# A launch with idle products and second-stage tables in two parts, in a kernel of a Fourier layer and a gated two-layer network

## The chip, the cores and the metric

The kernel runs on one core of a Trainium2 chip. The metric is the device time in microseconds (us). Differences are judged against executions of the kernel before on the same chip. TensorE does the matrix products, VectorE and ScalarE copy and compute, GpSimd and SyncE issue the loads and stores.

## The reference

For 8 batches of 3072 x 256 numbers, a real Fourier transform along the 3072, a complex 256 x 256 mixing with a bias and a shrinkage, the inverse transform, and then a gated two-layer network on neighbouring rows:

```python
X = np.fft.rfft(x, axis=1)
Yr = Xr @ w_r - Xi @ w_i + b_r
Yi = Xr @ w_i + Xi @ w_r + b_i
# shrink each by lam = 0.01
y = np.fft.irfft(Yr + 1j * Yi, n=x.shape[1], axis=1)
# the second half, on y as x
x_prev = x shifted by one row
k = np.maximum((mu_k * x + (1 - mu_k) * x_prev) @ w_k, 0.0)
out = sigmoid((mu_r * x + (1 - mu_r) * x_prev) @ w_r) * (k * k @ w_v)
```

## The kernel before

The transform is done in two stages by products with tables of sines: a first stage of 96 points, then (for the first two batches by "turns", which are products with an identity) a layout change, then a second stage with a table `G` that the kernel computes at launch. Then come the mixing (16 products per unit), the bias addition `z` with the shrinkage `Y` on VectorE, and the back products with an inverse table `GI`, which is `G` turned by TensorE. Six units `u` of four groups each make one batch.

A small scheduler in Python decides the order of instructions when the program is built: each unit has a due time and needs, copies are given to ScalarE or VectorE by which is estimated to be free first, and four slots of PSUM, the buffer that products are written to, are handed out. The resulting order on each engine is fixed; only the waits are decided on the chip.

The tables and the bias before the change (cuts are marked by dots, and some comments are added here):

```python
reduce_angle(scr[:, 768:2304], N, scr[:, 2304:3840])      # VectorE, 1536 elements
...
for src, p0, p1, g0, g1 in ((b_r, 0, 64, 0, 5), (b_i, 64, 128, 1, 5), (b_i, 65, 128, 0, 1), (b_r, 64, 65, 0, 1)):
    nc.gpsimd.dma_start(out=bias5[p0:p1, g0:g1, :], in_=src...to_broadcast(...))
...
def tables(k):                                            # two sines of 1536 elements
    nc.scalar.activation(G[:, :, :, 0, :], ang, AF.Sin, bias=0.0, scale=sc0)
    at(run_on("act", k, 1.5) + 0.3, tables1)
def tables1(k):
    nc.scalar.activation(G[:, :, :, 1, :], ang, AF.Sin, bias=0.0, scale=sc1)
    at(run_on("act", k, 1.5), tables2)
```

The mixing, what follows it on VectorE, and the back products:

```python
def shrink(k):
    nc.vector.tensor_scalar(out=y, in0=z, scalar1=LAM, scalar2=-LAM, op0=ALU.min, op1=ALU.max)
    nc.vector.tensor_tensor(out=y, in0=z, in1=y, op=ALU.subtract)
...
def back(u):
    def issue(ps, h, end):
        y = Y.pop(u)
        for i in range(4):
            nc.tensor.matmul(ps[:, 256 * i:256 * i + 256], GI[:, 4 * u + i, :],
                             y[:, 256 * i:256 * i + 256], start=True, stop=True)
...
units.append(Unit(f + g, 0.87, [("xt", b, u)] + ([("xt0", b), "bias"] if u == 0 else []), mix(u, 0)))
...
tab += [Unit(18.0 + n, 0.5, ["G", ("x1", 0, 3, 1)], table_gi(n)) for n in range(3)]
```

## Time and profile before

| what | before |
|---|---|
| median of 3 runs | 592.51 us (592.41 to 592.64) |
| span of the traced run | 591.0 us |
| busy: TensorE, VectorE, ScalarE | 96%, 88%, 71% |
| products of the input (128 x 96), mean | 280 ns |
| start of the first bias addition `z` | 25.01 us |
| first VectorE copy of batch 1's turns, "the hand-over" | 44.34 us |

The time is a few tenths of a per cent longer than the span, which runs from the first to the last instruction. The prediction shows the lines that carry most of this. Two more are needed later. The first is from the groups by shape of the kernel before, between 6 and 15 us. Its columns are line, engine, operation, output and inputs, shapes, type and count, then the busy time and the mean ns of one, then idle time before them and what ended it. The second is from its chain of waits (start, length, what).

```profile
L326 PE MATMUL banks<-FT,xs 96*128 96x96 f16 x64 | 5.9, 280 | 2.0 <-DMA xs<-in_x_dram 2.0
```

```profile
28.53 1.75 PE banks L414 x16
```

The input products are slow here: 280 ns each, where those of the same line and shape take 206 ns from 35.4 us on. A later mixing of 16 products takes 1.75 us, at a granted clock of 1.00.

### The profile page before, as it was taken

The numbers are of one execution on the slowest core, as the hardware profiler recorded it, in microseconds if no ns is written. First come the engines' busy times: TensorE is split into PE (matmuls) and PEld (weight loads), VectorE is DVE, ScalarE is ACT, GpSimd is POOL, SyncE is SP. The second block draws the span as 40 slices with busy tenths as digits, with TensorE's granted clock in tenths as the row PEclk, the third lists the DMA queues.
The fourth block names the chain that finished last, engine by engine and source line by source line (L and its number), as shares of the span: only waits on it lengthen the run. The fifth ranks groups of instructions, "written<-read, shape, count | busy, mean of one in ns | idle before, by whom it ended". The sixth has DMA issues, their size and how long they took to land.

```text
span 591.0 us, 12301 instructions
## 1 busy us (share of the span) xinstructions
PE 566.1 (96%) x4822; PEld 429.1 (73%) x4889; DVE 522.4 (88%) x831; ACT 421.0 (71%) x459; POOL 26.7 (5%) x56
## 2 busy tenths in 40 slices
PE   3999999999999999999999999999999999999996
PEld 3888666777767777677777777677876787776665
DVE  7799999789998899898998989988999889979883
ACT  5786967677768677676777677777776867767652
POOL 7101000000000000000000000000000000000000
PEclk9999999999999999999999999999999999999999
DMA  8976978724598265963478655683337722352223
GB/s 134 142 149 161 187 181 231 179 72 106 127 230 234 60 139 143 248 182 78 107 183 245 148 116 130 169 229 107 101 97 232 179 55 73 104 165 71 65 57 94
DMA packets 69594, 84.38 MB, mean 143 GB/s; under 512 B 9121, under 2 KB 54560, under 8 KB 69536
## 3 DMA queue, kind: packets, MB, share of 16 engines
q1 hardware_dynamic: 62912, 68.98, 41.7%
q0 software_dynamic: 6432, 14.36, 16.7%
q8 instruction: 38, 0.62, 0.4%
q10 hardware_dynamic: 192, 0.26, 0.2%
q14 instruction: 20, 0.16, 0.1%
HBM read 50.73 MB, written 47.19 MB: 166 GB/s over the span
## 4 chain that ended last, share of the span: by engine, by line
PE 84%; ACT 6%; DVE 4%; issue 2%; DMA 2%; POOL 0%; SPq 0%; DVEq 0%; POOLq 0%; ACTq 0%
PE banks L670 28%; PE banks L626 24%; PE banks L414 14%; PE banks L653 5%; PE banks L453 4%; PE banks L271 3%; PE banks L386 3%; ACT rl L632 3%; PE banks L534 2%; ACT rg L658 2%; DMA xs<-in_x_dram 1%; PE banks L344 1%; DVE YT L220 1%; DMA out_dram<-o 1%; DVE z L426 1%
## 5 line engine op out<-in xcount | busy, mean ns | idle before, releaser
L632 ACT ACTIVATE rl<-banks 128x1024 bf16<-128x1024 f32 x192 | 193.6, 1029 | 94.3 <-PE banks L626 88.5
L626 PE MATMUL banks<-xk,wk 128*128 128x512 bf16 x701 | 188.7, 379 | 5.3 <-DVE xk L599 0.7
L670 PE MATMUL banks<-wv,k 128*128 128x256 bf16 x1536 | 183.0, 272 | 0.4 <-ACT rl L632 0.3
L670 PEld LDWEIGHTS <-k 128*128 128x128 bf16 x1536 | 149.3, 98 | 29.1 <-issue 1.4
L638 DVE TENSOR_TENSOR k<-rl 128x1024 bf16<-128x1024 bf16 x192 | 130.3, 684 | 13.6 <-ACT rl L632 13.5
L626 PEld LDWEIGHTS <-wk 128*128 128x128 bf16 x768 | 73.9, 98 | 60.7 <-issue 3.1
L414 PEld LDWEIGHTS <-XT 128*128 128x128 bf16 x768 | 74.5, 98 | 16.1 <-DVE XT L396 0.7
L414 PE MATMUL banks<-wi,XT 128*128 128x256 bf16 x384 | 73.3, 273 | 0.1
L414 PE MATMUL banks<-wr,XT 128*128 128x256 bf16 x384 | 73.3, 272 | 0.1
L599 DVE SCALAR_TENSOR_TENSOR xk<-diff,muk,YT 128x512 bf16<-128x512 bf16 x96 | 69.0, 744 | 0.2
L599 DVE SCALAR_TENSOR_TENSOR xr<-diff,mur,YT 128x512 bf16<-128x512 bf16 x96 | 68.7, 744 | 0.0
L681 DVE TENSOR_TENSOR o<-banks,rg 128x1024 f32<-128x1024 f32 (+1 forms) x49 | 58.6, 1195 | 3.7 <-PE banks L670 3.4
L218 ACT ACTIVATE YT<-banks 128x768 bf16<-128x768 f32 x57 | 43.5, 830 | 11.3 <-PE banks L534 7.9
L218 ACT ACTIVATE XT<-banks 128x1024 bf16<-128x1024 f32 (+2 forms) x46 | 43.3, 950 | 10.4 <-PE banks L386 10.4
L653 PE MATMUL banks<-wrm,xr 128*128 128x256 bf16 x384 | 49.8, 272 | 0.1
L658 ACT ACTIVATE rg<-banks 128x1024 bf16<-128x1024 f32 x48 | 49.2, 1025 | 0.0
L431 ACT ACTIVATE z<-banks 128x1024 bf16<-128x1024 f32 x32 | 32.7, 1022 | 19.7 <-PE banks L414 19.6
L653 PEld LDWEIGHTS <-xr 128*128 128x128 bf16 x384 | 37.2, 98 | 11.6 <-issue 0.2
L218 ACT ACTIVATE V<-banks 128x1024 bf16<-128x1024 f32 x35 | 35.9, 1025 | 12.8 <-PE banks L453 12.8
L218 ACT ACTIVATE A<-banks 96x1024 bf16<-96x1024 f32 (+1 forms) x39 | 39.3, 1023 | 7.5 <-PE banks L271 6.2
L593 DVE TENSOR_TENSOR diff<-YT 128x1024 bf16<-128x1024 bf16 x48 | 32.8, 683 | 3.8 <-ACT YT L218 3.8
L220 DVE CAST A<-banks 96x1024 bf16<-96x1024 f32 (+1 forms) x21 | 25.5, 1221 | 11.4 <-PE banks L271 9.4
(90 smaller groups left out, 448.3 us busy)
## 6 DMA issues: line engine op xcount, KB each, us to landing
out_dram<-o SPq DMA_DIRECT2D x188, 128.0 KB, 2.3
xs<-in_x_dram POOLq DMA_DIRECT2D x32, 384.0 KB, 6.5
Vdr<-V SPq DMA_DIRECT2D x192, 64.0 KB, 1.8
V<-Vdr SPq DMA_DIRECT2D x32, 384.0 KB, 7.0
Adr<-A SPq DMA_DIRECT2D x24, 384.0 KB, 5.6
A<-Adr SPq DMA_DIRECT2D x48, 192.0 KB, 4.3
wk<-in_moe_w_k_dram POOLq DMA_DIRECT2D x1, 512.0 KB, 14.1
wv<-in_moe_w_v_dram POOLq DMA_DIRECT2D x1, 512.0 KB, 14.5
```

The lines of the kernel that those rows point to most:

```text
L218: nc.scalar.activation(out, in_, AF.Copy, bias=0.0, scale=1.0)
L414: nc.tensor.matmul(o, lhs, w[:, c, :], start=(w is wr and c == 0), stop=(w is wi and c == NCD - 1))
L431: nc.scalar.activation(z, ps, AF.Copy, bias=0.0, scale=1.0)
L593: nc.vector.tensor_tensor(out=df, in0=y, in1=yp, op=ALU.subtract)
L599: nc.vector.scalar_tensor_tensor(out=m[:, c, :], in0=df[:, c, :], scalar=mu[:, c:c + 1], in1=yp[:, c, :], op0=ALU.mult, op1=ALU.add)
L626: nc.tensor.matmul(ps[:, 512 * f:512 * f + 512], wk[:, c, 128 * ff:128 * ff + 128], xk[:, c, :], start=(c == 0), stop=(c == NCD - 1))
L632: nc.scalar.activation(rl, ps, AF.Relu, bias=0.0, scale=1.0)
L638: nc.vector.tensor_tensor(out=k2, in0=rl, in1=rl, op=ALU.mult)
L653: nc.tensor.matmul(ps[:, 256 * q:256 * q + 256], xr[:, c, 128 * q:128 * q + 128], wrm[:, c, :], start=(c == 0), stop=(c == NCD - 1))
L658: nc.scalar.activation(rg, ps, AF.Sigmoid, bias=0.0, scale=1.0)
L670: nc.tensor.matmul(ps[:, 256 * q:256 * q + 256], K2[t][:, ff, 128 * q:128 * q + 128], wv[:, ff, :], start=(ff == 0), stop=(ff == NCF - 1))
L681: nc.vector.tensor_tensor(out=o[:, lo:hi], in0=ps[:, lo:hi], in1=rg[:, lo:hi], op=ALU.mult)
```

## The change

The intent is to start the body earlier. Products of zeros ("idle products") keep TensorE busy from the launch so that its clock gate is open when the input arrives. By the clock gate I mean what the traces show as two speeds of TensorE, with a granted clock of 0.50 where it is shut and of 1.00 where it is open. In the kernel before, turns of one shape take 289 ns before 19.8 us and products of that shape 218 ns behind it. The opening is its first clock record, at 19.21 us. A gate that is still shut at the launch doesn't show in the granted clock: it reads 1.00 between 13 and 16 us, where the first turns took 305 ns. Half of the second-stage table, which is enough for the first three units, is made first. The other half, the three later turns and the inverse tables are put behind the first mixings. The core of the diff:

```diff
+    idle = const.tile([128, 512], BF16, name="idle")
+    nc.vector.memset(idle, 0.0)
+    def keep_warm(ps, n):
+        for _ in range(n):
+            nc.tensor.matmul(ps[:, 0:512], idle[:, 0:128], idle, start=True, stop=True)
...
-    reduce_angle(scr[:, 768:2304], N, scr[:, 2304:3840])
+    for o in (0, 768):
+        reduce_angle(scr[:, 768 + o:1536 + o], N, scr[:, 2304 + o:3072 + o])
...
+                if b == 0 and c == 1:            # in the pauses between input loads
+                    spare, i = take()
+                    keep_warm(spare, 2 if q < 3 else 1)
+                    release(i, end + 0.5)
...
+            if b == 0 and u > 2:                 # the last three turns wait
+                needs.append(("xt", 0, LATE[u - 3]))
...
+                    if b == 0 and u < 2:         # second half of the sines
+                        at(k, lambda k: tables3(k, u))
...
-                needs = [("y", b, u), "GI"]
+                needs = [("y", b, u), ("GI", u // 2)]
...
-    done["FT"], done["bias"] = 5.0, 21.0
+    done["FT"], done["bias"] = 5.0, 20.0
...
-    tab += [Unit(18.0 + n, 0.5, ["G", ("x1", 0, 3, 1)], table_gi(n)) for n in range(3)]
+    tab += [Unit(18.0 + 3 * n, 0.5, ["G1" if n else "G", ("mixed", 0, 2 * n)], table_gi(n)) for n in range(3)]
...
+    spare, i = take()
+    keep_warm(spare, 14)
+    release(i, 6.0)
```

More of the change, by code (lines that the diff above doesn't have):

```diff
@@ L195 @@
     heap, seq = [], itertools.count()
-    free = {"pe": 0.0, "act": 6.0, "dve": 12.0}
+    free = {"pe": 0.0, "act": 6.0, "dve": 12.7}
     done, slots = {}, {}
@@ L354, in issue @@
                 at(end, evac)
-            return Unit(t1 + (t2 - t1) * u / 6, 0.45, [("x1", b, 3, 0), ("x1", b, 3, 1)], issue)
+            needs = [("x1", b, 3, 0), ("x1", b, 3, 1)]
+            if b == 0 and u > 2:
+                needs.append(("xt", 0, LATE[u - 3]))
+            return Unit(t1 + (t2 - t1) * u / 6, 0.45, needs, issue)
         return [make(q, c) for q in range(4) for c in range(2)] + [turn(u) for u in range(NU)]
     NU = NG // 4
+    LATE = (0, 0, 1)
     def middle(b, t0, t1):
@@ L417, in issue @@
                     return
+                done["mixed", b, u] = end - 0.15
                 z = r1_pool.tile([128, 1024], BF16, name="z")
@@ L501, in middle @@
             if s < NU:
-                units.append(Unit(f, 0.44, [("A2", b, s), "G"], second(s)))
+                units.append(Unit(f, 0.44, [("A2", b, s), "G1" if s > 2 else "G"], second(s)))
             if 0 <= s - 1 < NU:
@@ L727, in evac, with sine @@
                                                 scalar2=None, op0=ALU.mult)
-                if n == 2:
-                    done["GI"] = e
+                done["GI", n] = e
             at(end, evac)
         return issue
+    def sine(hf, j):
+        g = slice(12 * hf, 12 * hf + 12)
+        nc.scalar.activation(G[:, g, :, j, :], ang[:, g], AF.Sin, bias=0.0, scale=(sc0, sc1)[j])
     def tables(k):
-        nc.scalar.activation(G[:, :, :, 0, :], ang, AF.Sin, bias=0.0, scale=sc0)
-        at(run_on("act", k, 1.5) + 0.3, tables1)
+        sine(0, 0)
+        run_on("act", k, 0.85)
+        at(11.6, tables1)
     def tables1(k):
-        nc.scalar.activation(G[:, :, :, 1, :], ang, AF.Sin, bias=0.0, scale=sc1)
-        at(run_on("act", k, 1.5), tables2)
+        sine(0, 1)
+        at(max(14.0, run_on("act", k, 0.85)), tables2)
     def tables2(k):
@@ L744, in tables2, with tables3 @@
         done["G"] = run_on("dve", k, 0.5)
+    def tables3(k, j):
+        sine(1, j)
+        e = run_on("act", k, 0.85)
+        if j == 1:
+            done["G1"] = e
     P = 71.5
@@ L781 @@
     for q in range(4):
-        done["x", 0, q] = 6.0 + 2.55 * q
+        done["x", 0, q] = (6.3, 8.9, 11.0, 12.8)[q]
         load_x(1, q)
@@ L788 @@
     big["wv"] = load_w("wv", moe_w_v, NCF, D)
-    done["FT"], done["bias"] = 5.0, 21.0
-    at(12.0, tables)
+    done["FT"], done["bias"] = 5.0, 20.0
+    at(10.9, tables)
     tab = [Unit(18.0, 0.1, ["FT"], table_fi)]
-    tab += [Unit(18.0 + n, 0.5, ["G", ("x1", 0, 3, 1)], table_gi(n)) for n in range(3)]
+    tab += [Unit(18.0 + 3 * n, 0.5, ["G1" if n else "G", ("mixed", 0, 2 * n)], table_gi(n)) for n in range(3)]
     streams = [tok, val, fa, fb, fc, tab]
     at(START - 10.0, lambda k: mix_tokens(0, k))
+    spare, i = take()
+    keep_warm(spare, 14)
+    release(i, 6.0)
     place, held, t = [0] * len(streams), {}, 0.0
```

## The prediction

> **What bounds the kernel now.** I read the page first. TensorE is busy 96% of 591.0 us and VectorE 88%, so the body is a TensorE pipeline. But the order of instructions of before and after is the same on TensorE, VectorE and ScalarE from the second batch's turns (about 42 us) to the end; only what stands before differs. So the whole effect is a shift of the moment at which that common order begins, and I read only the first 46 us, first in the chain of work that ended last:
>
> ```profile
> 4.10 8.63 DMA xs<-in_x_dram
> 12.77 1.47 PE banks L326 x16
> 14.34 0.97 DVE YT L220
> 15.35 4.18 PE banks L344 x39
> 19.56 0.69 ACT A L218
> ...
> 23.69 1.28 PE banks L414 x10
> 25.01 1.23 DVE z L426
> 26.24 0.02 issue
> 26.26 0.44 DVE Y L442
> 26.70 0.02 issue
> 26.72 0.70 DVE Y L443
> ...
> 43.16 1.13 DVE V L220
> 44.29 0.00 DVEq L220
> 44.29 0.04 issue
> 44.34 1.24 DVE A L220
> ```
>
> (Start, length, what.) The input lands at 12.73 whatever TensorE does. Then come the last first-stage products, the 48 turns (L344), the first mixing (L414), the first bias addition z at 25.01, and at 44.34 the first VectorE copy of batch 1's turns. That copy, 44.34, is the hand-over to the common order: I ask when it comes after the change.
>
> The groups of TensorE by shape, from the stretches 15 to 20 us and 20 to 24 us, show the clock:
>
> ```profile
> L344 PE MATMUL banks<-ident,YT 128*128 128x128 f16 x48 | 4.9, 289 | 0.8 <-ACT YT L218 0.7
> L716 PE MATMUL banks<-ident,G 128*128 128x128 f16 x24 | 1.7, 218 | 0.0
> ```
>
> The same shape takes 289 ns before 19.8 us and 218 ns behind it. The row of granted clock reads 9 everywhere, so it doesn't show this gate.
>
> Last the DMA issues of 5 to 23 us and GpSimd's timeline:
>
> ```profile
> bias<-in_b_i_dram POOLq DMA_DIRECT2D x1, 128.0 KB, 12.8
> bias<-in_b_i_dram POOLq DMA_DIRECT2D x1, 31.5 KB, 12.7
> bias<-in_b_r_dram POOLq DMA_DIRECT2D x1, 0.5 KB, 11.9
> 9.91 0.99 POOL L179 DMA_DIRECT2D bias<-in_b_r_dram  x1
> 21.50 0.73 POOL L170 DMA_DIRECT2D wrm<-in_moe_w_r_dram  x1 [3.79 <-DMA bias<-in_b_i_dram]
> ```
>
> The last number of an issue is the time from its start to its landing (for x: 4.10 + 8.63 = 12.73, and TensorE starts at 12.77). So the bias tile is complete at 9.91 + 11.9 = 21.8 us; GpSimd, which waits for one of its parts, goes on at 21.50. Before, nobody notices: z comes at 25.01.
>
> [...] L344 starts at 14.96 and the fast products start by 19.8; the earlier bursts (1.5 us with gaps of 0.3 to 1.3) did not open it. [...]
>
> **The change part by part.**
> *Idle products.* 14 products of 512 columns, from about 1.1 us (after one memset on an idle VectorE). [...] The first real product waits until 6.28 anyway, so they cost nothing. Two more fill each pause between the loads. If the gate is open at 12.77: 8 products of 96 columns take 0.51 us instead of 0.84 (rows of 35.4 and 9.7 us), so the last 16 end at 13.65, not 14.24. 48 turns at 56 ns instead of 104 ns would save 2.3 us, but only three of the six now stand ahead of the second stage.
>
> *Tables in two parts.* Two sines of 1536 elements (1.58 and 1.56 us) become four of 768, about 0.85 us each, two of them before the second stage. ScalarE has the last x1 copied at about 14.5; VectorE ends its share (copies 12.7 to 14.65, since the six passes of angle reduction together still end near 12.7), then G0 to 15.2. The turns start at 14.7 instead of 15.35. Turn 0 is computed at 15.3 and copied by ScalarE to 16.35; second stage 16.4 to 17.45, two more turns to 18.35; the negations on VectorE stand behind copies of 0.69 and 1.22 us and end at 19.15 and 19.4. The first mixing so ends about 20.3, against 24.97: 4.7 us earlier.
>
> *What this meets.* VectorE has one more copy in front (to 20.6) and could then do z. The bias is there at 21.8. No DMA issue in this stretch waits for work that the change speeds up (they wait for earlier landings), so I take 21.85 for z: 3.15 us earlier than 25.01, not 4.4.
>
> *What is moved behind z.* From z to the hand-over VectorE was busy with almost no pause, 25.01 to 44.34 = 19.3 us. In the order of after the same stretch holds: four z+Y+Y of 2.40 (9.6), two of them with z copied by ScalarE first, 1.8 each (3.6), the halving of GI 0.63, four negations of 0.23 (0.9), one turn copy 1.2, two V copies of 1.22 (2.45), three YT copies of 0.9 (2.7): 21.1 us. So 1.8 us of what used to stand before z now stands behind it. 21.85 + 21.1 = 42.95.
>
> *Waits inside.* TensorE has 24 inverse-table products (0.45 us a group of eight) and one turn in the way now, and four PSUM slots. Following the order by hand I find VectorE idle for about 0.1 us at a negation, 0.4 at the late turn (the third mixing waits for a slot first), 0.2 at the last z, and some 0.1 elsewhere: 0.8 us. Hand-over at 43.75 instead of 44.34: gain 0.6 us. ScalarE, by the same walk, is at its copy of batch 1 at 43.6 instead of 43.82: 0.2 us. So the sum: 4.7 earned, of which 1.5 lost to the bias wait and VectorE's copy, 1.8 to work moved behind, 0.8 to new pauses: 0.6 left. The stretch from 15 to 43 us is worked by hand, with an error of about 1 us, and the author of the change set the bias time to 20 in the schedule, which leans the other way; I move the point to a gain of 1.0: **591.5 us**.
>
> **The rivals.**
> *The bias is not in the way* (it lands earlier, or the first mixing comes later than I think). Then z is at 20.6 and the hand-over at 42.5: gain about 1.8, 590.7 us. For it: a change in order might shift DMA. Against: GpSimd's own wait at 21.50.
> *The whole 4.7 us comes through*, 587.8 us: if TensorE, not VectorE, set the pace from 25 to 44 us. TensorE is nearly full from 28 to 38 (5.00 and 4.88 of 5 us), which speaks for it; VectorE is at 4.95 of 5 in 40 to 45, and the chain there is VectorE, which speaks against.
> *The gate does not open early* (zeros don't count, or the pauses close it). Then the last first-stage products and three turns are slower by 0.6 + 1.2 us, z comes at about 22.4 instead of 21.85: gain 0 to 0.4, 592.3 us. Small, because the bias hides it.
> *New pauses are larger* (slots, inverse tables between back products): another 1 us, 592.9 us, about nothing gained or a little lost.
>
> **Range and chances.** My walk gives 591.9, the first rival 590.7, the full shift 587.8 at small odds, the pauses 592.9. Range 589.8 to 592.8. 2% would be 11.9 us, over twice all that the front could give (the input lands at 12.73 and 45 us is the hand-over), and nothing behind it changes order. Faster by over 2%: 0.01; within: 0.985; slower: 0.005.
>
> **What would show it.** Right: turns of about 218 ns from 14.7; the first mixing done near 20.3; z idle before it, released by the bias DMA, at 21.8; the first VectorE copy of batch 1's turns at 43 to 44; every later row moved by one constant. Wrong: L357 products at 289 ns; z before 21.5 or after 22.5; a hand-over before 42 or after 44.5; or a shift that grows or shrinks after 46 us (a DMA then sets the pace).

Where a cut is marked, the prediction told rules of the hardware that no run of this case shows. Two stand as my assumptions. One is that a waiting `z` holds up everything behind it on VectorE: in the trace of the changed kernel VectorE stands idle for the 1.85 us ahead of `z`, and its next piece of work starts at 23.68 us. The other is an end of the 14 idle products near 6 us: in that trace they end at 6.70 us, the first clock record (1.00) is at 5.90, the first input products start at 6.58 instead of 6.33, and the last ones at 12.76, where before it was 12.77. The 0.85 us for a sine of 768 elements is an estimate from the 1.58 and 1.56 us of the long ones; 0.94 and 0.92 were measured in the changed kernel. The sum: 4.7 less 1.5, 1.8 and 0.8 leaves 0.6 us, and the point was then moved to a gain of 1.0, which makes 591.5. A pause of TensorE that shuts the gate had no term in it.

## The result and the profile after

The changed kernel took 593.16 us (median of 6 runs, 592.70 to 595.16). The kernel before took 592.51 us in the same rounds (592.27 to 593.49). The ratio is 1.0016 with a 95% interval of 0.9999 to 1.0032. Ratios here are the mean time of one kernel's runs over that of the other's of the same rounds, so they are not quite the ratio of the medians quoted. The class "within 2%" was right. The point of 591.5 was not, and the median lies 0.36 us above the range. All outputs are right.

The six times are not one cluster: four lie at 592.70, 592.80, 593.12 and 593.20 us, and two at 594.45 and 595.16. The traced run is the one of 594.45. What its trace shows is therefore first of all the story of a slow one.

**The launch.** The groups by shape of the changed kernel, 0 to 15 us, show the input products:

```profile
L335 PE MATMUL banks<-FT,xs 96*128 96x96 f16 x64 | 3.4, 206 | 2.3 <-DMA xs<-in_x_dram 2.3
```

They take 206 ns instead of 280: the zeros opened the gate. But for one product at 14.25 us, the turns started at 14.85 us (predicted 14.7), and the first mixing ended near 20.4 us (predicted 20.3).

**The bias.** The timeline of the changed kernel (start, length, engine, line, operation, operands, count, then the idle time before it and what ended it) shows the first `z` on VectorE and the first back product on TensorE:

```profile
22.42 1.22 DVE L446 TENSOR_TENSOR z<-banks,bias 128x1024 bf16<-128x1024 f32 x1 [1.85 <-DMA bias<-in_b_i_dram]
...
25.27 0.60 PE L473 MATMUL banks<-Y,GI 128*128 128x256 bf16 x4 [2.08 <-DVE GI L746]
```

VectorE stands idle for 1.85 us until the bias lands, as predicted, but at 22.42 us rather than 21.85. The back product needs `Y`, which needs this `z`, and it also needs the halved row of `GI`, which VectorE does just behind `Y`. So TensorE has nothing to do for 2.08 us. Before, the first back product waited 0.30 us.

**What the pause did.** The chain of waits of the changed kernel (the part from the first `z` to the second inverse table, then the hand-over):

```profile
22.42 1.23 DVE z L446
23.68 0.44 DVE Y L462
24.14 0.69 DVE Y L463
...
25.27 0.60 PE banks L473 x4
25.87 0.45 PE banks L403 x8
26.31 3.22 PE banks L433 x16
29.53 0.65 PE banks L736 x8
...
45.75 1.24 DVE A L229
```

The third mixing (L433, the L414 of before) takes 3.22 us where the kernel before took 1.75 at the line shown above. The windows of the changed kernel tell why. The columns are the stretch, its length, busy us and instruction count of the engines PE, PEld, DVE, ACT and POOL, then the granted clock, the DMA share and GB/s:

```profile
24.00:25.00 1.00, 0.00 (x0) 0.00 (x0) 0.95 (x4) 0.00 (x0) 0.00 (x0) 1.00 1.01 199
...
26.00:27.00 1.00, 1.00 (x12) 0.79 (x10) 0.97 (x2) 1.00 (x2) 0.00 (x0) 0.69 1.13 215
27.00:28.00 1.00, 1.00 (x6) 0.74 (x5) 0.86 (x3) 0.84 (x1) 0.00 (x0) 0.50 1.17 225
...
29.00:30.00 1.00, 1.00 (x11) 0.88 (x10) 0.43 (x1) 0.00 (x0) 0.00 (x0) 0.60 1.13 229
30.00:31.00 1.00, 1.00 (x15) 0.89 (x13) 0.96 (x2) 0.80 (x1) 0.00 (x0) 1.00 1.05 208
```

The granted clock is 0.50 in the middle of it. In finer windows it fell between 26.2 and 26.6 us and was back at 29.8, a stretch of 3.4 us. The pause of 23.19 to 25.27 had closed the gate again. One of the products in this stretch, by shape, 26 to 30 us:

```profile
L433 PE MATMUL banks<-wi,XT 128*128 128x256 bf16 x8 | 2.5, 418 | 0.0
```

It takes 418 ns on average, where the page of the kernel before has 273 for its L414. In all, the hand-over came at 45.75 us, 1.41 later than before.

**Behind the hand-over.** The prediction said that every later row moves by one constant. I compared the start of the first and of the last row of differences (`diff`) in the body. The shift grew from 1.41 to 1.67 us: 0.26 us were added in one place, near 250 us, where TensorE waits for the inverse-stage input of a batch (the load of V) to land. The traced spans differ by 592.7 - 591.0 = 1.7 us.

### The profile page after: what moved, and what is told of

Same layout as the page of the kernel before. It is cut to its first block, busy times and chain, and to the rows that moved or that the text cites. A ratio compares the mean times of both kernels' runs of the same rounds, so it can differ in the third digit from the quotient of the medians.

```text
span 592.7 us, 12418 instructions
## 1 busy us (share of the span) xinstructions
PE 574.1 (97%) x4910; PEld 428.4 (72%) x4910; DVE 523.4 (88%) x837; ACT 421.5 (71%) x461; POOL 25.9 (4%) x56
## 4 chain that ended last, share of the span: by engine, by line
PE 82%; ACT 5%; DVE 4%; DMA 4%; issue 2%; POOL 1%; SPq 0%; DVEq 0%; POOLq 0%; ACTq 0%
PE banks L690 27%; PE banks L646 24%; PE banks L433 14%; PE banks L673 5%; PE banks L473 3%; PE banks L280 3%; PE banks L403 3%; PE banks L554 2%; ACT rl L652 2%; DMA bias<-in_b_r_dram 2%; DMA V<-Vdr 1%; ACT rg L678 1%; DVE YT L229 1%; ACT YT L227 1%; DMA out_dram<-o 1%
## 5 line engine op out<-in xcount | busy, mean ns | idle before, releaser
L646 PE MATMUL banks<-xk,wk 128*128 128x512 bf16 x768 | 193.2, 379 | 2.0 <-DVE xk L619 0.7
L433 PEld LDWEIGHTS <-XT 128*128 128x128 bf16 x768 | 75.1, 99 | 16.9 <-issue 0.7
L433 PE MATMUL banks<-wr,XT 128*128 128x256 bf16 x384 | 74.1, 275 | 0.4 <-ACT GI L740 0.2
L433 PE MATMUL banks<-wi,XT 128*128 128x256 bf16 x384 | 74.3, 276 | 0.0
L451 ACT ACTIVATE z<-banks 128x1024 bf16<-128x1024 f32 x34 | 34.7, 1022 | 20.9 <-PE banks L433 20.8
```

The lines of the kernel that those rows point to most:

```text
L433: nc.tensor.matmul(o, lhs, w[:, c, :], start=(w is wr and c == 0), stop=(w is wi and c == NCD - 1))
L451: nc.scalar.activation(z, ps, AF.Copy, bias=0.0, scale=1.0)
L646: nc.tensor.matmul(ps[:, 512 * f:512 * f + 512], wk[:, c, 128 * ff:128 * ff + 128], xk[:, c, :], start=(c == 0), stop=(c == NCD - 1))
```

## The experiments

After this comparison I held three views of the traced run's loss of 1.4 us at the hand-over. One is that the re-closed gate costs it. One rival is that the new order has put more work behind `z` than I counted. The other is that the late bias costs it. A later question was the wait near 250 us. The 16 runs below, three of them unaltered kernels once more, went on four chips, each beside its own runs of the kernel before. What was expected of each stands below, and it quotes the theories as they stood at that time.

For reading: "z" is the start of the first bias addition on VectorE, "hand-over" the first VectorE copy of batch 1's turns, "end shift" the start of the last `diff` row minus that of the traced kernel before. All are us.

| run | z | hand-over | end shift | median (range) | ratio [95%] |
|---|---|---|---|---|---|
| before, traced | 25.01 | 44.34 | 0 | 592.51 | |
| before_again | 24.75 | 44.08 | -0.29 | 592.55 (592.31 to 593.29) | 1.0005 [0.9992, 1.0018] |
| after, first set | 22.42 | 45.75 | +1.67 | 593.16 (592.70 to 595.16) | 1.0016 [0.9999, 1.0032] |
| after_again | 22.02 | 43.68 | -0.18 | 592.52 (592.17 to 592.98) | 1.0000 [0.9986, 1.0013] |
| after_third | 21.58 | 43.24 | -0.90 | 592.24 (591.95 to 594.42) | 1.0002 [0.9990, 1.0015] |
| gap_filled | 21.99 | 43.81 | +0.27 | 592.62 (592.14 to 593.07) | 0.9995 [0.9975, 1.0015] |
| half_filled | 21.93 | 43.59 | +0.09 | 592.53 (592.18 to 593.19) | 0.9999 [0.9986, 1.0012] |
| bias_early | 20.94 | 42.61 | -1.55 | 591.80 (591.25 to 592.32) | 0.9980 [0.9960, 1.0000] |
| tables_only | 22.29 | 43.96 | -0.38 | 592.61 (592.17 to 593.15) | 0.9996 [0.9974, 1.0017] |
| tables_bias | 22.23 | 43.90 | -0.24 | 592.68 (592.25 to 593.18) | 1.0000 [0.9987, 1.0012] |
| idle_only | 24.44 | 43.77 | +0.12 | 591.42 (591.01 to 594.22) | 0.9985 [0.9961, 1.0009] |
| order_undone | 23.18 | 44.30 | +1.17 | 594.10 (593.74 to 595.50) | 1.0030 [1.0017, 1.0042] |
| idle_more | 23.42 | 42.75 | -0.78 | 591.08 (591.04 to 592.09) | 0.9980 [0.9968, 0.9992] |
| warm_more | 20.91 | 42.58 | -1.13 | 591.41 (591.27 to 591.58) | 0.9982 [0.9970, 0.9994] |
| tile_only | 24.86 | 44.19 | -0.15 | 592.29 (591.65 to 592.98) | 0.9998 [0.9985, 1.0011] |
| zeros_scratch | 23.29 | 42.62 | -1.56 | 591.11 (590.54 to 594.33) | 0.9984 [0.9968, 1.0001] |
| after_scratch | 22.00 | 43.67 | -0.21 | 592.23 (591.60 to 592.61) | 0.9995 [0.9983, 1.0007] |
| warm_scratch | 21.07 | 42.74 | -0.28 | 591.77 (590.99 to 592.48) | 0.9988 [0.9976, 1.0000] |

The kernel before had medians of 592.57 to 592.79 in the jobs. The columns z to end shift are from one traced run each, so an end shift need not agree with the median.

### The pause in front of the first back product

**gap_filled** puts eight products of zeros into the slot of the first back product, ahead of it. They overwrite nothing that is needed.

```diff
                 y = Y.pop(u)
+                if b == 0 and u == 0:
+                    keep_warm(ps, 8)
```

> Changed kernel plus 8 idle products written into the slot of the first product of batch 0 that waits for y, just ahead of it, so TensorE has about 1.7 of its 2.08 us pause (23.19 to 25.27) filled. Theory (the pause closes the clock gate again and the half-speed mixing costs 1.65 us): the mixing products of 26 to 29 us take 0.38 us a pair, not 0.64; third z at about 27.9 instead of 29.57; hand-over (first VectorE copy of batch 1's turns) at 44.1 instead of 45.75; span about 591.0, ratio to before about 1.000. Rival (the late bias alone sets the hand-over and the slow stretch is absorbed behind it): hand-over stays within 0.3 of 45.75 and the span within 0.3 of 592.7.

Its timeline shows the filled pause and no idle time in front of the back product:

```profile
23.27 1.89 PE L77 MATMUL banks<-idle 128*128 128x512 bf16 x7
24.99 0.60 PE L475 MATMUL banks<-Y,GI 128*128 128x256 bf16 x4
```

(One of the eight is missing among the records.) The clock stayed at 1.00 from 22 to 31 us, and the hand-over came 43.81 - 21.99 = 21.82 us after z, against 45.75 - 22.42 = 23.33 in the traced run of the changed kernel. So 1.5 us of that run's loss belong to the closed gate. The time is level with before, as expected.

**after_again** and **half_filled** ask if the closing is the rule. The first is the changed kernel, unaltered. The second is gap_filled with 4 products instead of 8.

> The changed kernel unaltered, on the same chip as the next three, to see how often its gate closes. Theory (one closing of about 3.4 us at half clock takes 0.003 off the mean clock of 592 us): most of its runs show a mean clock of 0.997 or less, as five of the six before did; the trace again has the second-last third of the first batch's mixing at half clock; median 593.0 to 593.4. Rival (the profiled run was a rare one): clock 0.999 to 1.000 in most runs and a median within 0.2 of the kernel before.

> Changed kernel with 4 idle products (0.87 us) in the 2.08 us pause, so 1.2 us of it stay empty. Theory (the gate is judged by the idle part of a window of 3.4 us: 2.08 us, 61%, closed it; 1.16 us, 34%, at launch did not): 1.2 us leave it open; hand-over near 44.1, as with the pause filled, mixing pairs at 0.38 us. Rival (any pause of about a microsecond can close it): half clock between 26 and 30 us again and hand-over above 45.

The timeline of after_again, first on VectorE, then on TensorE, then VectorE at the hand-over:

```profile
22.02 1.23 DVE L446 TENSOR_TENSOR z<-banks,bias 128x1024 bf16<-128x1024 f32 x1 [1.45 <-DMA bias<-in_b_i_dram]
...
24.87 0.60 PE L473 MATMUL banks<-Y,GI 128*128 128x256 bf16 x4 [1.68 <-DVE GI L746]
...
43.68 2.35 DVE L229 CAST A<-banks 128x1024 bf16<-128x1024 f32 x2
```

The bias came 0.40 us sooner, the pause was 1.68 us instead of 2.08, the clock stayed at 1.00, and the hand-over came 21.66 us after z. The same gap is 21.66 in half_filled, 21.66 in the third set (below) and 21.67 in the other kernels with the order of the change and an open gate there. The traced run's 23.33 is 1.66 more: that is what the closing cost. A pause that leaves the gate open costs nothing here: it was 0.55 to 1.68 us at the same gap. The closing is not the rule, against what I expected; it hangs on some tenths of a microsecond in the landing of the bias. (The 3.4 us in the theory of half_filled are the length of the traced run's closing, from 26.38 to 29.79 us; that the gate goes by windows of this length was then a guess.) In half_filled only 0.55 us of the pause stayed empty, not the 1.2 us meant, so it doesn't test the theory of idle shares. The median of after_again is 592.52, level with before.

**after_third** is the changed kernel once more, on another chip.

> The changed kernel unaltered a third time. Theory (the pause before the first back product is the time from the end of the second mixing, 23.2, to the bias landing plus 2.85 us of VectorE; 1.68 us of it left the gate open, 2.08 closed it; how much of it falls in one window is chance): clock 0.999 or 1.000 where the pause stayed harmless, with a median of 592.3 to 593.2; if the trace shows half clock between 26 and 30 us its hand-over is 45.3 to 45.8, if not 43.6 to 44.2, nothing between.

The bias landed at 21.58 us, the pause was 0.63 us, and the hand-over came at 43.24. In this run the gate had closed at the launch instead, with a clock of 0.50 from 11 to 14 us. The turns were later, but `z` still waited 0.41 us for the bias, so this closing cost nothing at the hand-over. The six times again have an outlier, 594.42, at a mean clock of 0.997.

The mean clock of a run can't say which closing took place: 3.4 us at half clock make 3.4 x 0.5 / 592 = 0.003. Besides, the gate closes behind the last products in nearly every trace, up to 2.95 us before the end of the span (tables_bias), which takes up to 0.0025 off. So 0.997 is one closing somewhere, or almost the end alone, and 0.995 needs one ahead of the end. All six runs of the first set were at 0.995 or 0.997, and in five of them it isn't known where the gate was closed.

### The bias and the idle products, each alone

**bias_early** loads the bias for two of the five groups (less to fetch) and lets VectorE copy the rest, one instruction of 0.54 us.

```diff
-    ... in ((b_r, 0, 64, 0, 5), (b_i, 64, 128, 1, 5), (b_i, 65, 128, 0, 1), (b_r, 64, 65, 0, 1)):
+    ... in ((b_r, 0, 64, 0, 2), (b_i, 64, 128, 1, 2), (b_i, 65, 128, 0, 1), (b_r, 64, 65, 0, 1)):
+                    if b == 0 and u == 0:
+                        nc.vector.tensor_copy(out=bias5[:, 2:5, :], in_=bias5[:, 1:2, :].to_broadcast([128, 3, D]))
```

> Changed kernel with the bias loaded for two of its five groups only and copied on VectorE to the other three just before the first z. Theory (z waits 1.85 us for the bias, and the pause of TensorE that closes the gate follows from it): bias lands before 20.5; copy about 0.4 us; z at about 21.0 instead of 22.42; pause of TensorE before the first back product under 1 us, gate stays open; hand-over at 42.5 to 42.9; span 589.4 to 590.0, ratio to before about 0.997. Rival (VectorE's work behind z or the slots, not its start, set the hand-over): z earlier but hand-over no earlier than 44.

```profile
20.31 0.54 DVE L445 COPY bias<-bias 128x768 bf16<-128x768 bf16 x1
20.94 1.23 DVE L448 TENSOR_TENSOR z<-banks,bias 128x1024 bf16<-128x1024 f32 x1
```

In the timeline of bias_early, `z` no longer waits for a load. It starts at 20.94, 1.08 us before that of after_again, and the hand-over at 42.61 is 1.07 us before it: this gain comes through whole. The pause in front of the back product is 0.77 us, and the gate stays open. The bias loads took 6.9 to 7.7 us from issue to landing, where the first set's took 9.5 to 13.1.

**tables_only** is the changed kernel without any product of zeros, and **tables_bias** is the same with the cheap bias.

> Changed kernel without any idle product: only the tables in two parts and the moved inverse tables. The gate is shut until about 19 us as before. Theory (bias hides the launch): turns at 289 ns again, first mixing ends near 22 instead of 20.5, z still released by the bias at 22.3 to 22.5; no pause above 1 us in front of the first back product, so the gate does not close again; hand-over about 44.1, span about 591.0, better than the whole change. Rival (opening the gate at launch earns what it looks like): hand-over and span 1.5 to 2 us later than the whole change, 594 or more.

> The change without idle products but with the bias loaded for two of five groups and copied. With the gate shut at launch the first mixing ended near 22.2 (z at 22.29 in the run without idle products), so the bias is no longer what z waits for. Theory: z stays at 22.0 to 22.4, hand-over at 43.7 to 44.1, span about 590.6: an early bias is worth nothing without the idle products, and the idle products are worth 1.3 us with it (20.94 and 42.61 in the run with both). Rival (bias still holds z here): z at 21 to 21.6 and hand-over 43.2 or earlier.

Without the zeros, 16 input products take 1.46 us in tables_only, as in the kernel before, where they take 0.85 behind the zeros. The turns between 12 and 22 us take 285 and 274 ns on average, and `z` comes at 22.29 and 22.23, close to where the bias lets it start in the changed kernel. Both kernels are level with before, and the early bias alone is worth nothing: the mixing is not ready sooner.

**idle_only** is the kernel before with the zeros alone: 14 at the launch, and 2, 2, 2 and 1 in the pauses between the loads.

> Kernel before plus only the idle products (launch and between the loads), tables as before. Theory: turns at 218 ns from 14.8, copies of the turns wait for ScalarE's sines until 16.4, z at 23.6 to 24.0 (before 25.01), later than the bias, so the bias costs nothing; no new pause; hand-over 43.0 to 43.4 (before 44.34); span 589.7 to 590.2, ratio 0.998. Rival (VectorE and the sines set z whatever the clock): z within 0.3 of 25.01, span 591.

In the traced run, `z` came only 0.57 us before that of before, because the gate closed again during the launch. The windows of idle_only:

```profile
16.00:18.00 2.00, 2.00 (x22) 2.00 (x20) 1.58 (x5) 1.48 (x3) 0.46 (x1) 0.50 1.00 36
```

Two pauses for input, of 1.15 and 0.79 us, between 7 and 11 us were left in spite of the idle products, and the clock was at 0.50 from about 11.2 to 18.1 us. Four of the other runs took 591.0 to 591.5 us, so here the gain looks larger than in the changed kernel, with none of its table work, though the interval of its ratio reaches 1.0009. The traced run took 592.90, and one run took 594.22.

### The order of the late turns and the inverse tables

**order_undone** is the changed kernel with its split sines and zeros, but the late turns and the inverse tables are no longer held back behind the mixings.

```diff
-            if b == 0 and u > 2:
-                needs.append(("xt", 0, LATE[u - 3]))
-    tab += [Unit(18.0 + 3 * n, 0.5, ["G1" if n else "G", ("mixed", 0, 2 * n)], ...
+    tab += [Unit(18.0 + n, 0.5, ["G1" if n else "G", ("x1", 0, 3, 1)], ...
```

> Changed kernel (idle products, tables in two parts) with the new order undone: late turns and inverse tables ask for nothing but their inputs again, so they stand ahead of the first z as in the kernel before. Theory (what the change put behind z lies on VectorE, which is full until the hand-over; ahead of z there was a wait for the bias to use): z is later, about 23.4, but only 18.0 us of VectorE work and 0.6 of pauses follow; first VectorE copy of batch 1's turns at 41.9 to 42.6; span 589.0 to 590.0, ratio 0.996 to 0.998; no pause over 1 us on TensorE in 18 to 40 us. Rival (the order is right and only the gate and the bias cost): hand-over no earlier than 43.8, span 590.5 or more.

The first `z` at 23.18 us was as expected. The rest was not: the hand-over came 21.12 us behind it, not the 18.6 that I had counted. The timeline of TensorE and of VectorE shows two of the new pauses:

```profile
31.64 0.39 PE L431 MATMUL banks<-wi,XT 128*128 128x256 bf16 x2 [1.02 <-DVE XT L411]
...
33.38 1.23 DVE L444 TENSOR_TENSOR z<-banks,bias 128x1024 bf16<-128x1024 f32 x1 [1.59 <-PE banks L431]
```

The scheduler set a negation (L411) behind other VectorE work that it should have preceded, the mixing waited 1.02 us for it, and the next `z` waited 1.59 us for the mixing. TensorE also waited 1.77 us for a copy, from 19.47 to 21.23, and the gate stayed open; this is needed below. The order behind the hand-over changed too. At 594.10 us this is the one kernel clearly slower than before. It shows that the author's order is needed with the split tables, but not what the change would be worth with a better one. It is no clean test of the moved work.

### More idle products

**idle_more** is idle_only with 6, 4, 4 and 2 products of zeros in the pauses. **warm_more** is bias_early with the same.

```diff
-                    keep_warm(spare, 2 if q < 3 else 1)
+                    keep_warm(spare, (6, 4, 4, 2)[q])
```

> The kernel before with the idle products only, but 6, 4, 4 and 2 of them behind the input loads. Theory: its gate stays open at launch, which it did not in the traced run with the short fillers (half clock from 11.2 to 18.1 us): turns at 218 ns, first z at 23.4 to 24.0 instead of 24.44, hand-over at 42.8 to 43.4 instead of 43.77, median 591.0 to 591.6 without outliers above 592.5; ratio 0.9975 to 0.9985. Rival (the sines on ScalarE set the copies of the turns): z at 24.2 or later whatever the clock, median as with the short fillers.

> The changed kernel with the cheaper bias load, and 6, 4, 4 and 2 idle products behind the four input loads in place of 2, 2, 2 and 1, so no pause before 14 us is longer than about 0.4 us. Theory (the gate is judged by idle share, and with the short fillers the launch itself can close it, as in the trace with idle products alone): half clock nowhere before the end, all mean clocks 0.998 or more, first z at 20.8 to 21.0, hand-over at 42.5 to 42.7, median 591.2 to 591.8, no run above 592.6; ratio to before 0.998. Rival (more fillers delay the input products): z later than 21.3, median above 592.

The timeline of idle_more shows the turns on TensorE, and `z` and the hand-over on VectorE:

```profile
14.97 2.99 PE L355 MATMUL banks<-ident,YT 128*128 128x128 f16 x48 [1.09 <-ACT YT L225]
...
23.42 1.22 DVE L437 TENSOR_TENSOR z<-banks,bias 128x1024 bf16<-128x1024 f32 x1
...
42.75 2.36 DVE L227 CAST A<-banks 128x1024 bf16<-128x1024 f32 x2
```

The gate stays open, the 48 turns take 2.99 us in all, `z` is 1.59 us earlier than before, and the hand-over is 1.59 us earlier too. Both kernels are faster than before by a small margin (0.2%) whose interval excludes 1: 591.08 and 591.41 against 592.57 in the same rounds. idle_more has none of the table change. The traced run of idle_more was the slowest of its five (592.09), the other four took 591.04 to 591.21.

### The wait near 250 us

In eleven of the thirteen traces with idle products, 0.17 to 1.11 us are given back at one place, the load of V near 250 us; bias_early (0.02) and order_undone (0.00) are the exceptions. (The four kernels with the cheap bias, and they alone, give back another 0.2 us near 192 us, which was not followed up.) In the timeline of after_again and then of before:

```profile
250.42 1.02 PE L554 MATMUL banks<-FI,V 96*128 96x96 f16 x20 [0.71 <-DMA V<-Vdr]
```

```profile
251.12 0.50 PE L534 MATMUL banks<-FI,V 96*128 96x96 f16 x8 [0.24 <-ACT rl L632]
```

In after_again TensorE waits 0.71 us for the load. SyncE had held the fetch back for 4.3 us until the stores of V had landed, where the same wait took 1.1 us before. What this gives back, beyond before, is 0.26 us in the first set, 0.49 in after_again, 0.82 and 0.84 in gap_filled and half_filled, 0.70 in idle_only and 0.84 in idle_more. tables_only and tables_bias, which have no idle products, give back nothing here. One theory (A) was that the new tile of zeros shifts the addresses of other buffers. The rival (B) was that the earlier body, or the zeros themselves, bring it about. **before_again** is the kernel before, unaltered. **tile_only** is the kernel before with the tile and its memset but no product. **zeros_scratch**, **after_scratch** and **warm_scratch** are idle_more, the changed kernel and warm_more with their zeros in an unused part of a scratch buffer, so without the tile.

```diff
-    idle = const.tile([128, 512], BF16, name="idle")
+    idle = scs[:, 1024:1280].bitcast(BF16)
```

> The kernel before unaltered, for a second trace of it. In four of the changed traces TensorE waits 0.2 to 0.8 us more at about 250 us for the load of the third batch's inverse input, and gives back that much of its lead; the trace of before has no such wait. Theory A (that load lands when the memory lets it, and the earlier a kernel comes the more it waits): again no wait there, rows behind 250 us stand where they did to 0.2 us. Theory B (chance of the run): the wait appears here too, and rows behind 250 us are 0.2 to 0.9 us later than in the first trace. First z at 25.0, hand-over at 44.3 in both.

> The kernel before plus the zero tile and its memset, no product reads it. Theory A (the tile moves the later buffers, and the store and reload through memory at 235 to 250 us becomes slower): hand-over as before, 44.0 to 44.4, but rows behind 255 us 0.3 to 0.9 later than the rows ahead of it; median 592.8 to 593.4. Theory B (the products or the earlier start do it): no extra wait, one constant shift within 0.1, median as before.

> The kernel before plus idle products (6, 4, 4, 2 behind the loads) that read zeros from an unused part of a scratch buffer already there, so no buffer moves. Theory A: hand-over 42.6 to 42.9, lead of 1.5 to 1.7 kept to the end (no wait at 250), span 589.2 to 589.5 in the trace, median 590.2 to 590.8. Theory B: the wait of 0.6 to 0.9 at 250 stays as in the run with the new tile, median 591.0 to 591.3.

> The changed kernel with its idle products reading the scratch buffer instead of a new tile. Theory A: hand-over 43.2 to 43.8 (45.3 to 45.8 if the gate closes), and no loss of lead at 250 us: median 591.7 to 592.2, which is what the prediction's walk gave. Theory B: lead lost at 250 as before, median 592.2 to 593.2.

> The changed kernel with the cheap bias load, the longer fillers and the zeros in the scratch buffer. Theory A: hand-over 42.5 to 42.7, lead of 1.7 kept, median 590.5 to 591.0. Theory B: 0.3 to 0.7 of it lost at 250, median 591.2 to 591.6 as in the run with the new tile.

before_again and tile_only show no wait at that place. zeros_scratch gives back 0.17 us there, after_scratch 0.47 and warm_scratch 1.11. So the tile alone doesn't bring the wait about, and taking it away doesn't remove it: theory A falls. The times agree: zeros_scratch has 591.11 as idle_more has 591.08, and warm_scratch gained nothing on warm_more. An earlier body is not what decides: bias_early is among the earliest and gave back only 0.02 us, and the first set, later than before, gave back 0.26.

The traces show one thing more. SyncE holds the fetch back for 3.8 to 4.7 us in all thirteen traces with idle products and for 0.9 to 1.5 us in the five without. In all thirteen, a fetch of 16 KB of instructions (queue q8) starts 1.3 to 2.6 us before the last of four stores of V is issued, and this store lands 4.85 to 5.74 us after its issue. In the five, the same fetch starts 0.2 to 0.9 us behind that issue, and the store takes 2.8 to 3.2 us. Idle products add instructions to TensorE, which may be what moves the fetch. This fits all 18 traces, but no run moved the fetch alone, so it is not shown. How much the hold costs depends on more: in bias_early and order_undone V still landed in time.

## Why the prediction was wrong

**The launch and the bias: right.** The gate opened, the first mixing ended near 20.4 us (predicted 20.3; the last input products were to end at 13.65, and 13.61 was measured), and `z` waited for the bias DMA and for nothing else. The landing itself varied: `z` at 22.42, 22.02 and 21.58 us in three traced runs around my 21.85.

**Work moved behind z: right in size.** From `z` to the hand-over the order of before takes 19.33 us in every traced run that has it, and the order of the change takes 21.67, so the change puts 2.34 us more there. I had 1.8 for the work and 0.8 for new pauses. From the kernel before to after_again, VectorE's busy time in this stretch grew by 1.53 us (18.56 to 20.09) and its idle time by 0.81 (0.77 to 1.58), so the pauses were right and the work 0.3 too high. With an open gate, `z` at 22.02 gave 43.68 at the hand-over, and the walk of the prediction had 43.75. That it came so near is in part luck: the bias was 0.17 us later than assumed and the stretch 0.23 shorter than my 21.9.

**The step that failed first** is that the pause of TensorE behind a waiting `z` got no term in the sum. I had taken it that such a pause leaves the gate open, which no run had shown. A pause of 2.08 us did close the gate in the traced run, for 1.66 us at the hand-over. Pauses of 1.68 us and less in the same place did not (after_again, after_scratch, after_third). The clock records in the trace files give the times of the changes. In each of the 18 traces every change of the granted clock lies a whole number of 3.413 us from every other: in the first set they are at 5.90, 26.38 and 29.79 us (6 and 1 times 3.413 apart), in the kernel before at 19.21 and 589.23 (167 times). Cut into windows at these instants, TensorE's idle share is:

| trace | window, us | idle | longest pause in or across it, us | gate after it |
|---|---|---|---|---|
| first set | 22.97 to 26.38 | 60.8% | 2.08 | closed |
| after_third | 7.25 to 10.66 | 51.8% | 1.35 | closed |
| idle_only | 7.80 to 11.21 | 51.4% | 1.15 | closed |
| after_scratch | 8.32 to 11.73 | 50.6% | 1.59 | open |
| after_again | 22.99 to 26.40 | 49.1% | 1.68 | open |
| order_undone | 17.28 to 20.69 | 35.7% | 1.77 | open |

So it isn't the length of one pause: 1.77 us, of which 1.22 lie in this window, left the gate open, and two pauses of which the longer was 1.35 closed it. The first three are all the closings ahead of the end; the others passed with the most idle time or with the longest pause. The idle share of a window fits these six: 51.4% and more closed it, 50.6% and less did not. It isn't a sharp limit: behind the last products, windows of 53.5% (first set) and 54.5% (idle_only) still left the gate open, so the profile's idle time alone does not decide it.

My own estimate of the bias landing said that a pause would come, since TensorE had nothing else to do between the second mixing and the first back product. At my 21.85 for `z` it would have been about 1.5 us (21.85 + 2.85 - 23.19), which the other traces let pass; the landing 0.57 us later made it 2.08.

**The sum of the traced run.** The walk had 43.75 us. The bias came 0.57 us later than assumed, the closed gate took 1.66, and the stretch behind `z` was else 0.23 shorter than my 21.9: 43.75 + 0.57 + 1.66 - 0.23 = 45.75, which is what the trace shows. Near 250 us come 0.26 more.

**"Every later row moved by one constant" failed too.** Up to 0.84 us are given back near 250 us in kernels close to the change, and 0.22 and 0.49 in the two repeats of the change itself. This place alone takes up about the gain that the walk had at the hand-over (0.6 us). I had read only the first 46 us.

**Moving the point from 591.9 to 591.5** because the walk was done by hand and the author's assumption leaned the other way went in the wrong direction. The walk was off by 0.07 us at the hand-over in after_again, and what it had left out (the closing, the loss near 250 us) pointed to slower.

**What the miss of 0.36 us is made of.** Without its closing, the traced run of 594.45 would be at 592.8, where the other four of the lower cluster lie (592.7 to 593.2). The median of the six would then be 592.96, still 0.16 above the range, so this one closing doesn't account for the whole miss. So the ordinary execution of the change is level with before: the gain of 0.66 us at an ordinary hand-over (44.34 - 43.68) less some tenths near 250 us. In the two repeats, the medians of 592.52 and 592.24 lie inside my range. That the first median falls outside it comes from a lower cluster that was itself a little high and two slow executions above it. One of the two is shown to have the closed gate in its pause. For the other, and for the height of the lower cluster, the cause stays open: outliers above 594 us occur in idle_only, in zeros_scratch and in the kernel before (596.28, clock 0.996) as well, and one of 594.42 in after_third.

**Where the gain of the launch went.** Zeros alone, with the old order, give 1.59 us at `z` and all of it at the hand-over (idle_more). The tables in two parts with the new order make `z` 2.72 us earlier without zeros (tables_only), but give 2.34 of it back right behind. With the zeros as well, the bias holds `z` at 21.58 to 22.42. By the medians, the two parts together are worth less than the zeros alone. Relieved of the bias wait (bias_early, warm_more) the changed order is about level with idle_more, so the split isn't harmful, but it pays for nothing that zeros didn't already buy.

## What to carry to other kernels

Making the start of a chain earlier is worth only what is left when the next release, here a bias load that nobody had noticed before, and the work that was moved behind the start are taken off. Before a change lengthens a pause of TensorE, put idle products into it or give the closing of the clock gate a chance and a price, here 1.66 us at the hand-over for a pause of 2.08 us: it decides between two times, so the prediction should be a mixture and not a point. The gate closed here behind windows of 3.413 us that were 51.4 to 60.8% idle; less than half of each window idle is the safer aim that these runs suggest. Try the cheapest part of a change alone, since here it beat the whole.
